# Attention and experts of a fused kernel: other homes for the state product, the fills, the splits and the router's numbers; conversion in half pieces, second half by row blocks

## The chip, the cores and the metric

The kernel runs on one core of one Trainium2 chip. The time is the device time of one execution in microseconds (us); a kernel is measured as the median of several runs. The core's engines are TensorE (PE in the profile, its weight loads PEld), VectorE (DVE), ScalarE (ACT), GpSimd (POOL) and SyncE (SP), which starts most DMAs. Products go from TensorE to the banks of PSUM; everything else lies in SBUF.

## The reference

Three layers stand one behind the other. The first is a gated linear recurrence over 768 steps for 2 x 8 heads of 40 numbers, the second a router with two of eight experts for 1,536 tokens of 320 numbers, the third a dense block with a SoLU, a norm and two more products.

```python
for t in range(S):                                  # attention, per batch and head
    m_new = max(f_gate + m, i_gate)
    f_stab, i_stab = exp(f_gate + m - m_new), exp(i_gate - m_new)
    C = f_stab * C + i_stab * outer(vt, kt); n = f_stab * n + i_stab * kt
    y[t] = sigmoid(o_gate) * (C @ qt) / max(abs(n @ qt), 1)
logits = x @ w_gate + log1p(exp(x @ w_noise)) * noise     # router, 8 experts
out[mask] += top2_w * (maximum(x[mask] @ w1[e], 0) @ w2[e])
h = x @ w_in; solu = h * softmax(h)                 # last block
return layer_norm(solu) * g_ln @ w_out
```

## The kernel before

**Attention** works in 12 tiles of 128 steps; tile i is of batch i % 2. Within a tile the recurrence is a masked product of scores, and the state `CC` carries what went before. One turn of the loop (line 684, i = 4 to 10) mixes work of several tiles: the router's ranks of tile i - 3, its numbers for tile i - 2, the rows of tile i - 1, the scores and keys of tile i + 1. `keys` gives GpSimd the product `qa` of the queries with the decay `A`, and VectorE the weighted keys `kw`. `update` multiplies keys and values to the bank `U`; `state` multiplies the old state by the decay of the tile's last step (line 388, on VectorE, `CC<-CC,A`) and adds the two halves of `U` (line 392). The next `update` may write the bank only behind those adds. `causal` masks a tile's `E` on GpSimd; `send` scatters a tile's rows to their experts by two indirect DMAs on GpSimd's queue.

**Fills** are matmuls on constant data, whose result nobody reads; in the prologue (up to 48.5 us: tiles 0 to 3, written out by hand in lines 531 to 682) they stand between the steps on TensorE. They write the columns 328 to 511 of the bank that `U` has at that moment.

**The router.** `trans` turns the rows into the bank pT (one buffer), `logits` writes 16 columns of it, `route_act` copies them to `lg` and takes a log of the noise half, `route` works on 8 numbers a token on VectorE, `slot` finds the place of the row. `weave` takes one step of each of several such chains in turn.

**Weights** come as f32 and are split into a high and a low part (`split_hi` on ScalarE, `split_lo`, line 121, on VectorE or GpSimd); a layer is then three matmuls for one. A raw tile `r0` to `r6` (0 to 2 are w1 by 1,024 columns, 3 to 6 are w2 by 640) may be loaded for the next expert (`load_w`) once both parts are made. The splits of expert 0 stand in the loop. Behind the loop (to 137.5 us) come the last tile's rows and router, and layer 1 and two of eight slices of layer 2 of expert 0's first 192 rows (`early_mm`, `early_cut`, `early_out`), then a branch on a count (line 801).

**An expert** (137.5 to 350.5 us, eight of them) has a first half, eight slices f of layer 1, each cut to high and low by ScalarE and VectorE (`cut_h`, lines 139 to 142), and a second half, layer 2 (lines 149 to 154), which runs over the slices f and within each over the row blocks n of 128 rows. Behind it `put` takes each block from PSUM (line 164) and scatters it. The last block's weights are 64-bit floats; `convert` makes f32 of them on VectorE, six pieces of 1,024 columns (w_out first), one step a slice in the second halves of the experts 1 to 6, over one buffer each of the raw tile `R`, `u`, `sc` and `sq`; the result in `u` is stored to DRAM (line 948). In code order the engines' queues are fixed; nothing is scheduled anew.

Of the kernel before, what the change touches and what calls it, by code (L numbers as in the profile page):

```python
# [36 lines left out]
def fused_kernel(ctx: ExitStack, tc, qt, kt, kv, og, ig, fg, wgn, noise, w1, w2, win, wout, gln, cst, out):  # L37
# [154 lines left out]
    with ExitStack() as pa:  # L192
# [56 lines left out]
        held = dict(U=pw)  # L249
# [132 lines left out]
        def state(i):  # L382
# [3 lines left out]
            Co, Cn, U = CC[b][c % 2], CC[b][(c + 1) % 2], T[i]["U"]  # L386
            if c > 0:
                ve.tensor_mul(Cn, Co, T[i]["A"][:, :, P - 1 : P].to_broadcast([P, 4, 82]))
# [39 lines left out]
        def route_act(i):  # L428
            lg = T[i]["lg"] = a2.tile([P, 16], F32, tag="lg", name=f"lg{i}")
            act.activation(lg, T[i]["pT"][:, 3, 0:16], AF.Copy)  # L430
            z = T[i]["z"] = a2.tile([P, NE], F32, tag="z", name=f"z{i}")
            act.activation(z, lg[:, 8:16], AF.Exp)
            act.activation(z, z, AF.Ln, bias=1.0)

        def route(i):
# [5 lines left out]
            yield ve.tensor_mul(z, z, noise_s[:, i])  # L441
            yield ve.tensor_add(z, z, T[i]["lg"][:, 0:8])
# [93 lines left out]
        fill(6)  # L536
# [3 lines left out]
        fill(6)  # L540
        for j in range(2):
            decays(1, j)
        fill(6)
# [17 lines left out]
        fill(8)  # L561
# [27 lines left out]
        fill(6)  # L589
        attend(0)  # L590
        fill(4)
# [21 lines left out]
        fill(6)  # L613
        trans(0)
        fill(4)
# [25 lines left out]
        fill(6)  # L641
        attend(2, 4, 8)
        fill(6)
# [34 lines left out]
        fill(6)  # L678
# [5 lines left out]
        for i in range(4, NTILE - 1):  # L684
# [13 lines left out]
            for j in (i - 5,) if i in (5, 7, 9) else (6,) if i == 10 else ():  # L698
                split_lo(0, j, pool)
# [8 lines left out]
            for j in (i - 5,) if i in (6, 8) else (5,) if i == 9 else ():  # L708
                split_lo(0, j, ve)
# [14 lines left out]
            for j in ((0, 1), range(2, 7))[i - CUT - 1] if i > CUT else ():  # L724
                load_w(1, j)
        t = NTILE - 1
# [24 lines left out]
        weave(route(t - 1))  # L751
        early_mm(0)
# [4 lines left out]
        weave(slot(t - 1))  # L757
        send(t - 1)
# [543 lines left out]
```

## Time and profile before

| what | before |
|---|---|
| median of 3 runs | 458.82 us (456.35 to 461.11) |
| profiled execution | 459.58 us, of which the span is 457.5 |
| mean granted clock of TensorE | 0.948 |
| busy: PE, DVE, ACT, POOL | 433.5 (95%), 297.1 (65%), 238.9 (52%), 191.8 (42%) us |
| DMA | 71.73 MB, 157 GB/s over the span |
| stages, us from the start | prologue to 48.5, loop to 106.8, behind it to 137.5, experts to 350.5, last block to 457.5 |

The busy share says which engine has the most work over all stages, not which one is waited for. The granted clock is the share of TensorE's full clock that the chip allowed in a stretch: 1.00 is 2.4 GHz, 0.50 is 1.2 GHz. In a row of instructions, the bracket is the engine's idle time just before it and who ended that.

### The profile page before, as it was taken

Reading aid. Unit: us, or ns where it says so; the run is one execution under the profiler, and the core shown is the slowest. Engines: PE = TensorE matmul, PEld = TensorE weight load, DVE = VectorE, ACT = ScalarE, POOL = GpSimd, SP = SyncE. Lnnn points to the kernel's source line nnn. Section 1 sums busy time; section 2 is a strip of 40 time slices with the busy share of each in tenths; the row PEclk is TensorE's granted clock in tenths of the full one; section 3 lists DMA queues with packets and bytes.
Section 4 is the critical chain, followed back from the end, with each engine's and each line's share of the span. In section 5 each row is a group of like instructions: output and inputs, shape, how many; then the busy total and the mean of one; then the engine's idle time right before and its main releaser. Section 6 shows DMA issues by size and latency. Waiting matters only on the chain.

```text
span 457.5 us, 8125 instructions
## 1 busy us (share of the span) xinstructions
PE 433.5 (95%) x2777; PEld 407.1 (89%) x2777; DVE 297.1 (65%) x722; ACT 238.9 (52%) x517; POOL 191.8 (42%) x277
## 2 busy tenths in 40 slices
PE   7998979999989999999999969979999999999996
PEld 4887979998978989899999969969999789989996
DVE  8696698797446558575647665486355877556541
ACT  4687574661327362644626156236382776665542
POOL 8534666676317250541807218045203253342340
PEclk9999785896599999999999998989999999999999
DMA  6777894664424947375483834834602411120001
GB/s 187 245 225 219 295 273 133 229 239 148 179 85 143 323 135 271 125 239 181 129 302 91 319 113 137 295 101 127 211 1 102 147 45 43 45 85 16 29 16 43
DMA packets 36094, 71.73 MB, mean 157 GB/s; under 512 B 4225, under 2 KB 18981, under 8 KB 35408
## 3 DMA queue, kind: packets, MB, share of 16 engines
q1 hardware_dynamic: 32896, 62.06, 42.3%
q0 software_dynamic: 2912, 8.68, 5.2%
q8 instruction: 24, 0.39, 0.4%
q10 hardware_dynamic: 240, 0.41, 0.3%
q14 instruction: 22, 0.18, 0.1%
HBM read 55.50 MB, written 16.21 MB: 157 GB/s over the span
## 4 chain that ended last, share of the span: by engine, by line
PE 51%; DVE 9%; DMA 5%; issue 3%; ACT 1%; DVEq 0%; ACTq 0%
PE cpo L1173 3%; PE cpo L1175 3%; PE cpo L1174 3%; PE ph L127 3%; DMA wi<-cvu 3%; PE po L149 3%; PE po L150 3%; PE po L151 3%; PE pz L1165 2%; PE ph L128 2%; PE ph L133 2%; PE ph L130 2%; PE ph L132 2%; PE ph L129 2%; PE ph L131 2%
## 5 line engine op out<-in xcount | busy, mean ns | idle before, releaser
L166 POOL DMA_INDIRECT yt<-YS,ti x29 | 28.9, 995 | 126.4 <-DVE YS L164 119.8
L140 DVE SCALAR_TENSOR_TENSOR h<-ph,h 128x384 fp32r<-128x384 f32 (+1 forms) x64 | 34.3, 537 | 39.6 <-ACT h L139 39.5
L121 POOL TENSOR_TENSOR w0l<-r,w0h 128x1024 fp32r<-128x1024 f32 x23 | 54.7, 2408 | 9.8 <-ACT w0h L117 9.5
L139 ACT ACTIVATE h<-ph 128x448 fp32r<-128x448 f32 (+6 forms) x64 | 32.0, 503 | 48.1 <-PE ph L134 47.5
L149 PE MATMUL po<-w1h,h 128*128 128x320 f32 x184 | 56.8, 308 | 0.0
L151 PE MATMUL po<-w1h,h 128*128 128x320 f32 x184 | 56.7, 308 | 0.0
L150 PE MATMUL po<-w1l,h 128*128 128x320 f32 x184 | 56.7, 308 | 0.0
L476 POOL DMA_INDIRECT xg<-x,slots x24 | 25.8, 1075 | 27.6 <-DVE ix L444 12.5
L149 PEld LDWEIGHTS po<-w1h,h 128*128 128x128 f32 x184 | 34.6, 188 | 0.0
L150 PEld LDWEIGHTS po<-w1l,h 128*128 128x128 f32 x184 | 34.6, 188 | 0.0
L151 PEld LDWEIGHTS po<-w1h,h 128*128 128x128 f32 x184 | 34.6, 188 | 0.0
L340 PE MATMUL S<-Qb,Kb 128*128 128x128 f32 x192 | 32.9, 310 | 0.0
L127 PE MATMUL ph<-XH,w0h 128*128 128x448 f32 (+6 forms) x64 | 24.5, 383 | 7.9 <-DVE h L142 4.8
L121 DVE TENSOR_TENSOR w1l<-r,w1h 128x640 fp32r<-128x640 f32 x34 | 31.3, 934 | 0.4 <-ACT w1h L117 0.4
L937 ACT ACTIVATE cvq<-cvR 128x1024 f32<-128x1024 f32 (+1 forms) x6 | 6.3, 1052 | 46.0 <-DMA cvR<-in_win_dram 27.2
L1167 DVE TENSOR_TENSOR ZL<-pz,ZH 128x512 fp32r<-128x512 f32 x24 | 15.4, 685 | 22.6 <-ACT ZH L1166 22.6
L1173 PE MATMUL cpo<-w1h,ZH 128*128 128x320 f32 x96 | 30.0, 312 | 0.0
L1175 PE MATMUL cpo<-w1h,ZL 128*128 128x320 f32 x96 | 29.7, 309 | 0.0
L1174 PE MATMUL cpo<-w1l,ZH 128*128 128x320 f32 x96 | 29.7, 309 | 0.0
L117 ACT ACTIVATE w0h<-r 128x1024 fp32r<-128x1024 f32 x27 | 28.2, 1051 | 0.0
L340 PEld LDWEIGHTS S<-Qb,Kb 128*128 128x128 f32 x192 | 27.6, 214 | 0.1
L380 PE MATMUL Y<-KV,E 128*128 128x41 f32 x192 | 27.0, 296 | 0.0
(266 smaller groups left out, 1262.2 us busy)
## 6 DMA issues: line engine op xcount, KB each, us to landing
r<-in_w_dram SPq DMA_DIRECT2D x24, 512.0 KB
r<-in_w_dram SPq DMA_DIRECT2D x32, 320.0 KB
E<-gd SPq DMA_DIRECT2D x8, 512.0 KB
X<-xg SPq DMA_DIRECT2D x7, 579.0 KB
KV<-in_kv_dram SPq DMA_DIRECT2D x12, 324.0 KB
cY<-yt SPq DMA_DIRECT2D x12, 320.0 KB
cvR<-in_win_dram SPq DMA_DIRECT2D x3, 1024.0 KB
cvR<-in_wout_dram SPq DMA_DIRECT2D x2, 1024.0 KB
```

The source lines that it names most:

```text
L121: eng.tensor_sub(splits[e][2 * m + 1][:, k : k + n], raws[e, j], splits[e][2 * m][:, k : k + n].bitcast(F32))
L127: pe.matmul(ph, W1H[:, 0, fs], XH[:, 0], start=True, stop=False)
L139: act.activation(h[:, 0:n], ph, AF.Relu)
L140: ve.scalar_tensor_tensor(h[:, n + r : n + r + w], ph[:, 0:w], 0.0, h[:, 0:w].bitcast(F32), op0=ALU.max, op1=ALU.subtract)
L149: pe.matmul(po, hh, W2H[:, f], start=a, stop=False)
L150: pe.matmul(po, hh, W2L[:, f], start=False, stop=False)
L151: pe.matmul(po, hl, W2H[:, f], start=False, stop=z)
L166: i = pool.indirect_dma_start(out=yt, out_offset=bass.IndirectOffsetOnAxis(ap=idx[0:w], axis=0), in_=YS[0:w], in_offset=None, bounds_check ...
L340: pe.matmul(S[:, a], Kb[i % 3][j][:, a], Qb[i % 3][:, a], start=True, stop=True)
L1173: pe.matmul(po, ZH[:, f], W2H[:, f], start=(f == 0), stop=False)
L1174: pe.matmul(po, ZH[:, f], W2L[:, f], start=False, stop=False)
L1175: pe.matmul(po, ZL[:, f], W2H[:, f], start=False, stop=(f == 7))
```

## The change

Attention: the state product goes from VectorE (in `state`) to GpSimd (in `keys`, a turn earlier). The 64 fills of 184 columns become 18 of 448: the first six in the warm-up's tile pw, the others in tiles of their own in the banks `pr` and `D`. `lg` is gone: `route_act` writes its logs to the bank pT, and `route` reads pT. Of the splits of expert 0, GpSimd makes the three of w1 in turns 5, 7 and 9, and VectorE the four of w2 behind the loop, each followed by the load of the next expert's piece (`split2`). Four slices of `early_out` go from behind the branch to ahead of it.

Experts: conversion in 11 pieces of 512 columns, `R`, `u` and `sq` with two buffers, pieces loaded two ahead; two pieces in each of the experts 1 to 6. The second half of the first seven experts runs over row blocks and within each over the slices; `put` follows each block, and ScalarE evicts the full ones. In code behind that, the last expert takes the names of the new buffers for its own tiles.

The fills:

```diff
-        held = dict(U=pw)
-        def fill(n):
+        def fill(n, tag="U"):
+            w = pw if tag == "U" else ps1.tile([P, 512], F32, tag=tag, name="fill")
             for _ in range(n):
-                pe.matmul(held["U"][:, 328:512], warm[:, 0:P], warm[:, 0:184], start=True, stop=True)
+                pe.matmul(w[:, 0:448], warm[:, 0:P], warm, start=True, stop=True)
...
-        fill(6)
+        fill(2)
...
-        fill(6)
+        fill(2, "pr")
...
-        fill(6)
+        fill(2, "D")
```

Keys, update, state:

```diff
                 pool.tensor_mul(T[i]["qa"], Qb[i % 3], T[i]["A"])
+                if c < NC - 1:
+                    pool.tensor_mul(CC[b][(c + 1) % 2], CC[b][c % 2], T[i]["A"][:, :, P - 1 : P].to_broadcast([P, 4, 82]))
...
-                held["U"] = ps1.tile([P, 512], F32, tag="U", name=f"U{i}")
-                U = T[i]["U"] = held["U"][0:104, 0:328].rearrange("p (a d) -> p a d", d=82)
+                U = T[i]["U"] = ps1.tile([P, 4, 82], F32, tag="U", name=f"U{i}")[0:104]
...
-            if c > 0:
-                ve.tensor_mul(Cn, Co, T[i]["A"][:, :, P - 1 : P].to_broadcast([P, 4, 82]))
```

Router:

```diff
-            lg = T[i]["lg"] = a2.tile([P, 16], F32, tag="lg", name=f"lg{i}")
-            act.activation(lg, T[i]["pT"][:, 3, 0:16], AF.Copy)
-            act.activation(z, lg[:, 8:16], AF.Exp)
-            act.activation(z, z, AF.Ln, bias=1.0)
+            act.activation(z, T[i]["pT"][:, 3, 8:16], AF.Exp)
+            act.activation(T[i]["pT"][:, 3, 32:40], z, AF.Ln, bias=1.0)
...
-            yield ve.tensor_mul(z, z, noise_s[:, i])
-            yield ve.tensor_add(z, z, T[i]["lg"][:, 0:8])
+            yield ve.tensor_mul(z, T[i]["pT"][:, 3, 32:40], noise_s[:, i])
+            yield ve.tensor_add(z, z, T[i]["pT"][:, 3, 0:8])
```

Splits of expert 0, in the loop and behind it:

```diff
-            for j in (i - 5,) if i in (5, 7, 9) else (6,) if i == 10 else ():
-                split_lo(0, j, pool)
+            if i in (5, 7, 9):
+                split_lo(0, i // 2 - 2, pool)
...
-            for j in (i - 5,) if i in (6, 8) else (5,) if i == 9 else ():
-                split_lo(0, j, ve)
...
+        def split2(j):
+            split_lo(0, j, ve)
+            load_w(1, j)
...
         weave(route(t - 1))
+        split2(3)
...
         weave(slot(t - 1))
+        split2(4)
...
         weave(rows2(t), route(t))
+        split2(5)
...
         weave(slot(t), totals())
+        split2(6)
...
+        for f in range(2, 6):
+            early_out(f)
```

Experts:

```diff
-        cvs = (3, 4, 5, 0, 1, 2)
+        CW = 512
+        cvs = [(wo32, wout, c) for c in range(0, 8 * DM, CW)] + [(wi32, win, c) for c in range(0, 3 * DFF, CW)]
...
+                R = raw[i] = b1.tile([P, CW, 2], I32, tag=f"R{i % 2}", name=f"cvR{i}")
...
-            u = b1.tile([P, DFF], I32, tag="u", name=f"cvu{i}")[:, :n]
+            u = b1.tile([P, CW], I32, tag=f"u{i % 2}", name=f"cvu{i}")
...
-            if i != cvs[-1]:
-                load_raw(cvs[cvs.index(i) + 1])
+            load_raw(i + 2)
...
-                put_y((e, n, 1), YS[n], pos[n], T3, X[e]["ti"][:, n : n + 1], ws[n] < P, act if n == 2 and e + 1 < NE else ve)
+                put_y((e, n, 1), YS[n], pos[n], T3, X[e]["ti"][:, n : n + 1], ws[n] < P, act if e + 1 < NE else ve)
...
-                for f in range(8):
-                    for n in range(len(ws)):
                         layer2(pos[n], splits[e], hs[f], f, n, n_e)
-                    if e > 0:
-                        next(cv, None)
-                    if f % 2 == 0:
-                        split(3 + f // 2)
-                for n in range(len(ws)):
+                cv = chain(*(convert(i) for i in range(2 * e - 2, min(2 * e, len(cvs))) if e > 0))
+                for n in range(len(ws)):
+                    for f in range(8):
                         layer2(pos[n], splits[e], hs[f], f, n, n_e)
+                        s = 8 * n + f
+                        if s % 3 < 2:
+                            next(cv, None)
+                        q = 6 if e > 0 else 3
+                        if s % q == 0 and s < 4 * q:
+                            split(3 + s // q)
                     put(n)
```

GpSimd in turn 7 of the loop, between its constant copy for one tile's rows and the mask. Before, with `qa` of tile 8, a split of expert 0 and the two scatters:

```order
L401 COPY x_1110<-consts 128x1
L350 TENSOR_TENSOR qa_1156<-Qb_149,A_1025 128x512
L121 TENSOR_TENSOR w0l_244<-r_2_873,w0h_243 128x1024
L475 MEMSET nop 1x1
L476 DMA xg<-x_892,slots 12288x386
L475 MEMSET nop 1x1
L476 DMA xg<-x_892,slots 12288x386
L333 AFFINE_SELECT E_976<-E_976 128x1024
```

And now:

```order
L400 COPY x_1058<-consts 128x1
L350 TENSOR_TENSOR qa_1104<-Qb_149,A_976 128x512
L352 TENSOR_TENSOR CC_160<-CC_159,A_976 128x328
L121 TENSOR_TENSOR w0l_244<-r_1_723,w0h_243 128x1024
L472 MEMSET nop 1x1
L473 DMA xg<-x_845,slots 12288x386
L472 MEMSET nop 1x1
L473 DMA xg<-x_845,slots 12288x386
L333 AFFINE_SELECT E_929<-E_929 128x1024
```

The state product stands between `qa` and the split (piece 1 of w1 where it was piece 2), with nothing between the three.

VectorE behind the loop, from the end of tile 10's `route` through its `slot` to tile 11's `route` (`sk`, `sf`, `slots`, then `z`). Before:

```order
L447 TENSOR_TENSOR mk_1625<-oh_1624 128x8
L448 TENSOR_TENSOR cum_93<-cum_92,mk_1625 128x8
L458 TENSOR_TENSOR sk_1663<-oh_1624,pr_1651 128x16
L459 TENSOR_REDUCE sf_1664<-sk_1663 128x2
L460 CAST slots<-sf_1664 128x2
L410 COPY x_1584<-x_1584 128x64
L441 TENSOR_TENSOR z_1648<-z_1648,noise_s 128x8
```

And now, where `r_3` and `r_4` are raw tiles of w2 of expert 0:

```order
L444 TENSOR_TENSOR mk_1551<-oh_1550 128x8
L445 TENSOR_TENSOR cum_93<-cum_92,mk_1551 128x8
L121 TENSOR_TENSOR w1l_246<-r_3_935,w1h_245 128x640
L455 TENSOR_TENSOR sk_1590<-oh_1550,pr_1578 128x16
L456 TENSOR_REDUCE sf_1591<-sk_1590 128x2
L457 CAST slots<-sf_1591 128x2
L121 TENSOR_TENSOR w1l_246<-r_4_1041,w1h_245 128x640
L409 COPY x_1510<-x_1510 128x64
L438 TENSOR_TENSOR z_1575<-pT_1542,noise_s 128x8
```

Two splits of 640 columns stand between these steps; the third stands behind tile 11's `route`, the fourth behind its `totals`. And `z` is read from pT.

VectorE at the end of one expert's second half and the start of the next (`h_0` and `h_1` are the first two cut slices). Before:

```order
L946 SCALAR_TENSOR_TENSOR cvu_3510<-cvs_3511,cvu_3510 128x1024
L947 SCALAR_TENSOR_TENSOR cvu_3510<-cvq_3512,cvu_3510 128x1024
L121 TENSOR_TENSOR w1l_3341<-r_6_3320,w1h_3340 128x640
L938 TENSOR_SCALAR cvu_3617<-cvR_3571 128x1024
L164 COPY YS_0_3494<-po_0_3490 128x320
L164 COPY YS_1_3495<-po_1_3491 128x320
L162 TENSOR_TENSOR YS_3_3497<-po_3_3493,T_3498 64x320
L140 SCALAR_TENSOR_TENSOR h_0_3656<-ph_0_3647,h_0_3656 128x384
L142 SCALAR_TENSOR_TENSOR h_0_3656<-ph_0_3647,h_0_3656 128x64
L140 SCALAR_TENSOR_TENSOR h_1_3669<-ph_1_3660,h_1_3669 128x384
```

And now:

```order
L943 SCALAR_TENSOR_TENSOR cvR_3847<-cvR_3847,cvs_4126 128x512
L944 TENSOR_TENSOR cvs_4126<-cvR_3847,cvs_4126 128x512
L947 SCALAR_TENSOR_TENSOR cvu_4125<-cvs_4126,cvu_4125 128x512
L121 TENSOR_TENSOR w1l_3907<-r_6_3858,w1h_3906 128x640
L948 SCALAR_TENSOR_TENSOR cvu_4125<-cvq_4127,cvu_4125 128x512
L162 TENSOR_TENSOR YS_3_4063<-po_3_4059,T_4064 64x320
L140 SCALAR_TENSOR_TENSOR h_0_4231<-ph_0_4222,h_0_4231 128x384
L142 SCALAR_TENSOR_TENSOR h_0_4231<-ph_0_4222,h_0_4231 128x64
L140 SCALAR_TENSOR_TENSOR h_1_4244<-ph_1_4235,h_1_4244 128x384
```

The two evictions of `po` are gone from VectorE's order, and so is the first operation of the next piece, which stood between the split and the evictions; the last operations of a half piece (512 columns) stand in its place.

## Rows read from the trace of the kernel before

**Rows 1.** Windows: us; busy us (count) of PE, PEld, DVE, ACT, POOL; PEclk, DMA share, GB/s

```profile
13.00:45.60 32.60, 29.00 (x271) 28.04 (x270) 24.78 (x71) 23.49 (x64) 13.88 (x21) 1.00 0.78 234
48.47:106.81 58.34, 55.11 (x409) 54.11 (x408) 50.25 (x172) 34.88 (x102) 37.81 (x48) 0.82 0.67 218
106.81:137.46 30.65, 28.55 (x170) 26.87 (x169) 15.46 (x91) 8.21 (x30) 10.77 (x21) 0.72 0.45 149
137.46:350.45 212.99, 204.97 (x1239) 196.09 (x1238) 131.83 (x256) 103.47 (x176) 81.26 (x80) 0.98 0.54 177
86.00:93.00 7.00, 7.00 (x65) 6.92 (x64) 5.44 (x26) 5.90 (x18) 3.89 (x6) 1.00 0.77 255
```

**Rows 2.** Windows, the stretches at half clock, columns as before

```profile
45.70:52.50 6.80, 6.30 (x34) 6.20 (x34) 3.85 (x22) 3.85 (x14) 4.37 (x8) 0.50 1.07 336
66.20:83.20 17.00, 16.68 (x81) 16.57 (x82) 14.40 (x50) 9.04 (x26) 10.11 (x12) 0.50 0.60 183
107.20:124.20 17.00, 17.00 (x80) 15.75 (x79) 9.34 (x49) 4.82 (x19) 8.32 (x16) 0.50 0.59 208
274.40:277.80 3.40, 3.40 (x12) 3.38 (x11) 1.71 (x6) 0.94 (x2) 2.93 (x6) 0.50 0.38 136
305.10:308.40 3.30, 3.30 (x12) 3.30 (x11) 1.52 (x3) 1.44 (x2) 2.84 (x6) 0.50 0.37 127
```

**Rows 3.** Waits of TensorE: engine, line, waited for, us in total, times, longest

```profile
PE ph L127 <- DVE h L142: 4.8, 3, 3.9
...
PE epo L149 <- PEq L801: 2.0, 1, 2.0
...
PE U L256 <- DVE CC L394: 1.5, 2, 1.0
```

**Rows 4.** Timeline: start, us, engine, line, operation, out<-in, shapes, count [idle before, ended by]

```profile
46.20 1.08 PE L256 MATMUL U<-warm 128*128 128x184 bf16 x6 [2.68 <-DVE CC L392]
...
62.50 3.27 DVE L388 TENSOR_TENSOR CC<-CC,A 128x328 f32<-128x328 f32 x1
...
64.15 1.25 POOL L350 TENSOR_TENSOR qa<-Qb,A 128x512 f32<-128x512 f32 x1
...
66.52 1.68 PE L367 MATMUL U<-KV,kw 128*104 128x82 f32 x8 [2.48 <-DVE CC L392]
```

**Rows 5.** Timeline of the experts, VectorE and TensorE around two waits for h

```profile
266.97 0.69 DVE L938 TENSOR_SCALAR cvu<-cvR 128x1024 int32<-128x1024 int32 x1 [6.64 <-DMA wi<-cvu]
267.58 0.82 DVE L121 TENSOR_TENSOR w1l<-r,w1h 128x640 fp32r<-128x640 f32 x1
...
274.06 0.42 PE L127 MATMUL ph<-XH,w0h 128*128 128x396 f32 x1 [3.89 <-DVE h L142]
...
304.39 0.44 PE L127 MATMUL ph<-XH,w0h 128*128 128x384 f32 x1 [3.09 <-DVE h L140]
```

**Rows 6.** Line 388: engine op xcount: ns min/median/max, first and last start, forms

```profile
L388 DVE TENSOR_TENSOR CC<-CC,A x8: 488/944/3278, 32.6 to 98.9; 128x328 f32<-128x328 f32 x8
```

**Rows 7.** Timeline of the prologue, the transposes of tile 1 and the add of tile 0's route

```profile
36.60 0.49 PE L416 MATMUL pT<-consts,x 128*128 128x128 f32 x3
...
36.90 0.16 DVE L442 TENSOR_TENSOR z<-z,lg 128x8 f32<-128x8 f32 x1
```

**Rows 8.** Timeline of TensorE in the loop, the update of two turns

```profile
87.37 0.88 PE L367 MATMUL U<-KV,kw 128*104 128x82 f32 x8
...
93.83 0.88 PE L367 MATMUL U<-KV,kw 128*104 128x82 f32 x8
```

**Rows 9.** Groups by shape, GpSimd, 46 to 106 us: count | busy us, mean ns | idle before

```profile
L121 POOL TENSOR_TENSOR w0l<-r,w0h 128x1024 fp32r<-128x1024 f32 x2 | 4.7, 2352 | 4.1 <-ACT w0h L117 4.1
```

**Rows 10.** Timeline of expert 0: two matmuls of layer 2, and the last slice's cut

```profile
169.87 0.30 PE L149 MATMUL po<-w1h,h 128*128 128x320 f32 x1
...
170.31 0.31 PE L149 MATMUL po<-w1h,h 128*128 128x320 f32 x1
...
170.65 0.56 DVE L140 SCALAR_TENSOR_TENSOR h<-ph,h 128x384 fp32r<-128x384 f32 x1 [0.64 <-ACT h L139]
```

More of the change, by code (lines that the diff above doesn't have):

```diff
@@ L539, in fused_kernel @@
         gates2(0, 1)
-        fill(6)
+        fill(2)
         for j in range(2):
             decays(1, j)
-        fill(6)
+        fill(2)
         exps(0)
@@ L560, in fused_kernel @@
         update(0)
-        fill(8)
         scores(1, 0)
@@ L588, in fused_kernel @@
         probs(1, 1)
-        fill(6)
+        fill(2, "pr")
         attend(0)
-        fill(4)
+        fill(2, "pr")
         for j in range(2):
@@ L612, in fused_kernel @@
         attend(1, 4, 8)
-        fill(6)
+        fill(2, "pr")
         trans(0)
-        fill(4)
         transc(0)
@@ L640, in fused_kernel @@
         attend(2, 0, 4)
-        fill(6)
+        fill(2, "D")
         attend(2, 4, 8)
-        fill(6)
+        fill(2, "D")
         trans(1)
@@ L677, in fused_kernel @@
         attend(3, 4, 8)
-        fill(6)
+        fill(2, "D")
         load_d(7)
@@ L723, in fused_kernel @@
                 early_load()
-            for j in ((0, 1), range(2, 7))[i - CUT - 1] if i > CUT else ():
+            for j in ((0, 1), (2,))[i - CUT - 1] if i > CUT else ():
                 load_w(1, j)
+        def split2(j):
+            split_lo(0, j, ve)
+            load_w(1, j)
         t = NTILE - 1
@@ L995, in prep_x @@
                 ve.tensor_sub(v["H"][64:128, d, 0:r], pt[64:128, 0:r], v["T"][64:128, 0:r].bitcast(F32))
-        def conversions():
-            for i in cvs:
-                yield from convert(i)
         X[0] = dict(x=rest, n=CAP - EARLY, w=[P] * ((CAP - EARLY) // P))
@@ L1008, in fused_kernel @@
         T3 = b1.tile([P, DM], F32, tag="T3", name="eT3")
-        for f in range(2, 8):
+        alloc_x(0)
+        for d in range(3):
+            prep_x(0, d)
+        for f in range(6, 8):
             early_out(f)
-            if f == 2:
-                alloc_x(0)
-            if f == 5:
-                for d in range(3):
-                    prep_x(0, d)
         for n in range(2):
             put_y((0, n), YS[n], early["po"][n], T3, eti[:, n : n + 1], n == 1, ve)
-        cv = conversions()
         for e in range(NE):
@@ L1041, in fused_kernel @@
                 if e == 0 and f == 7:
-                    load_raw(cvs[0])
+                    load_raw(0)
+                    load_raw(1)
                 if e + 1 < NE:
@@ L1070, in fused_kernel @@
             else:
-                tags = dict(Y="R", x2="u", XH="sc", XL="sq", T="T", pt="pt")
-                held = {}
+                tags = dict(Y=("R0", "R1", "Y2"), x2=("u0", "u1"), XH=("sq0",), XL=("sq1",), T=("T",), pt=("pt", "pt"))
                 def newb(t):
-                    def new(k, shape, dt):
-                        if k not in ("Y", "x2"):
-                            return (pst if k == "pt" else b1).tile(shape, dt, tag=tags[k], name=f"c{k}{t}")
-                        if k not in held:
-                            held[k] = b1.tile([P, 3 if k == "Y" else 2] + shape[1:], dt, tag=tags[k], name=f"c{k}")
-                        return held[k][:, t]
-                    return new
+                    return lambda k, shape, dt: (pst if k == "pt" else b1).tile(shape, dt, tag=tags[k][t], name=f"c{k}{t}")
                 for n in range(4):
```

19 lines of the change are left out of this document (8 added, 11 removed).

## The prediction, made before the change was run

> **What bounds the kernel now.** I read four views in this order. First, the busy time and granted clock by stage: in the experts (137.5 to 350.5 us) the profile has TensorE busy for 205.0 of 213.0 us at a mean clock of 0.98, while in the attention loop (48.5 to 106.8) the clock is 0.82 and in the stretch behind it (to 137.5) 0.72 [rows 1]. So TensorE sets the pace everywhere, but in attention it does so at half clock for much of the time: three stretches of 6.8, 17.0 and 17.0 us lie at 0.50, which is the 1.2 GHz level, and two of about 3.4 us lie in the experts, at 274.4 and at 305.1 [rows 2]. A half-clock stretch that TensorE fills costs half its length.
>
> Second, what TensorE waited for: nearly only VectorE. In the experts it waited for the cut of a hidden slice (`h`): 4.8 us in three waits [rows 3] and 3.09 in one that ended at 304.39 [rows 5]. In attention it waited for the state's add `CC`: 1.5 us in two waits ahead of the loop [rows 3], 2.68 us before 46.20 and 2.48 before 66.52 [rows 4]. So four of the five half-clock stretches begin at a long wait or within a microsecond of its end: 46.20, 66.52, 304.39, and 3.89 us before 274.06 [rows 5]; the third does not.
>
> Third, why VectorE was late. In attention it was the product `CC<-CC,A`, line 388, both of whose inputs lie in SBUF: 0.49 us at the least and 3.28 at the most [rows 6]. The one at 62.50 took 3.27 us; it ended 0.37 us after GpSimd's product `qa`, which had begun 1.65 us later [rows 4]. In the experts it was the conversion: at 266.97 VectorE had stood for 6.64 us because the next piece writes the one buffer `u` whose store to DRAM was still under way. Behind it in VectorE's order stood splits, two evictions of `po` and then the cut of `h`, so TensorE's layer 1 went on only at 274.06 [rows 5].
>
> **The change, part by part.**
>
> *Ahead of the loop.* Fills now write other banks (`pr`, `D`) than the U bank that the state add reads, so the waits of 1.5 us (two) and 2.7 us in front of fills go [rows 3, 4]. What comes next there is data that is ready: E of tile 0, x, logits. One new wait comes: `route` now reads its numbers from the one-buffer bank pT, so the transposes of tile 1 must wait for the add in `route(0)`, which ended at 36.90 + 0.16 = 37.06, where they began at 36.60 [rows 7]: 0.5 us, with scores of tile 4 queued behind. Fills come to 18 x 448 = 8,064 columns for 64 x 184 = 11,776; the 3,712 that go are 1.5 us at 2.4 GHz, a gain only where TensorE sets the pace, and VectorE is busy for 24.8 of 32.6 us beside it [rows 1], so I count them at nothing. Term: -4.2 + 0.5 = **-3.7**; bounds -5.2 (with the columns) and 0 (the other chains of the prologue take it all).
>
> *The loop, seven turns, 58.3 us.* At full clock a turn takes 93.83 - 87.37 = 6.46 us [rows 8], so seven take 45.2, the floor. The state product leaves VectorE (eight, 0.49 to 3.28 us) for GpSimd. GpSimd's price is bounded by its product over 512 columns (1.25 us, [rows 4]) and by nothing; in proportion 328 columns are 0.8 us, and I take 0.85, nearer to that row. GpSimd is busy 37.8 us in the loop [rows 1]; it gains five products (4.3) and a split of 1024 columns (2.35, [rows 9]), and loses one of 640 (in proportion about 1.5): 42.9, or 6.1 a turn, under 6.46 as a mean. In the turns 5, 7 and 9, which have a split, it has about 1.3 us more than a turn; causal masks are made a turn ahead, which covers one such turn but not three in full. So I take 48 us for the loop: the floor of 45.2 and 0.9 for each of those three. The wait of 2.5 us for the U bank goes with the long product, since the adds that free the bank (line 392) read PSUM and one SBUF tile. Term: 58.3 - 48 = **-10.3**; bounds -13.1 (floor) and -2 (one 17 us stretch at half clock again, 8.5).
>
> *Behind the loop, 30.7 us.* Four splits of 640 columns now stand in VectorE's order between route, slot and totals; undisturbed one takes 0.82 us [rows 5], together 3.3. VectorE is busy there for 15.5 of 30.7 us [rows 1], so they fit, yet they lie on the chain to the cuts that TensorE's `early_mm(6)` waits for. At half clock TensorE is the slower and they cost nothing; at full clock TensorE would be 8.5 us earlier, less some 2.5 of those splits, which gives -6. The stretch at half clock began here with no long wait ahead of it, only with small matmuls, and those stay; but VectorE comes in without the two delayed splits in turns 8 and 9. Between -6 and 0 I take **-2**, nearer to the row as it stands. The weight loads of expert 1 for layer 2 move behind these splits on SP's queue; they are wanted only in expert 0's second layer, over 10 us later. Four of the six early slices of layer 2 (20 matmuls, 2.9 us) move ahead of the branch; TensorE stands at it for 2.0 us [rows 3] wherever it comes, so this is a swap: 0. If the branch could hide behind them, -2.
>
> *Experts.* `u`, `sq` and the raw tile get two buffers, and raw pieces are loaded two ahead, so the wait for the store and the wait for the load go. Two half pieces are the work of one whole one plus seven more starts, on an engine that is busy 131.8 of 213.0 us there [rows 1]. Evictions of `po` go to ScalarE, one after each row block, so they no longer stand between VectorE and the next `h`. What is late next? A second half is 88 matmuls of 0.147 us = 12.9 us [rows 10]. Two half pieces are seven operations on 1024 columns in sum, between 0.69 us (the first of them) and twice that each: 5 to 10 us, and four splits 3.3 [rows 5]. At the upper bound VectorE ends some 0.4 us late, and the next `h` is wanted only three slices into the next layer 1: it fits. The row-block order asks for the last slice after 21 matmuls, 3.1 us; VectorE finished it at 171.2 with 169.87 as the start [rows 10], 1.3 us in. So all four waits go: 4.8 + 3.1 = 7.9, and with them the two half-clock stretches, half of 6.8 = 3.4. Term **-11.3**; bounds -11.3 and -4 (each second half waits one us for its last slice).
>
> *The two-input price.* The row of 3.27 us says: a VectorE operation with two SBUF inputs waits while GpSimd works back to back [rows 4]. Two such stay in each turn (`kw`, and x from nm and den). I add **+1.5** for them (bounds 0 and 8.4, below).
>
> *Sum.* -3.7 - 10.3 - 2 - 11.3 + 1.5 = -25.8 on the profiled execution's 459.58: 433.8. The runs' median, 458.82, lies 0.8 below it: **433**.
>
> The Trainium skill, "SBUF — State Buffer", section "Who interferes with whom", has a rule that speaks against this change: a VectorE instruction with two SBUF inputs contends with a GpSimd instruction that reads SBUF, and the later one is blocked in full. The rows of line 388 agree with it. By that rule the product on GpSimd does not end the contention but hands it to the next two-input operation, which would bring the sum to the time of rival 1 instead of 433.
>
> **Rivals.**
>
> 1. *GpSimd's longer run blocks VectorE again.* In turns 5, 7 and 9 GpSimd does `qa`, the new product and a split end to end: 1.25 + 0.85 + 2.35 = 4.4 us. A `kw` or an x that arrives at its start waits that long; VectorE's own work in a turn without such a wait is 5.4 us less the product's 0.5 [rows 1, 6], so some 1.6 us of a turn is slack. Three times (4.4 - 1.6) is 8.4 us: 433 + 8 - 1.5 = about 440; with one 17 us stretch at half clock after it, 449. For: line 388 shows the wait. Against: the product that waited stood in VectorE's order right before GpSimd's run of mask and `qa`, while `kw` and x stand earlier in a turn.
>
> 2. *All at full clock behind the loop too*: tail -6 and loop at its floor: 433 - 4 - 3 = 426; with the branch hidden, 424.
>
> 3. *Thin fills, slower.* Now the clock is full ahead of 45.6 us [rows 1]. If the thinner fills let it fall behind the third group of them, at 13 us, the 29.0 us of TensorE work from there to 45.6 [rows 1] would take twice as long: +29, less 2 us that TensorE waits anyway, so with the prologue's gain gone 433 + 4 + 27 = about 464, slower than before. It decides once more than 26 us of work runs at half clock. Against: the waits beside the fills go, so the stretch is fuller than before though its fills are fewer.
>
> 4. *Row blocks stall every second half; no change.* In the old order the last slice is wanted only in the last eighth of a second half, in the new one after 3.1 us of it. If VectorE brought it 3.6 us later than in the row at 170.65, TensorE would wait 1.8 us in each of seven second halves (12.6), and if each wait were followed by a half-clock stretch like that at 274.4 (half of 3.4 us, times seven, 11.9), the sum is 433 + 24.5 = about 457. For: a longer wait stood ahead of such a stretch at 274. Against: VectorE's order ahead of that cut holds no conversion.
>
> **How the numbers follow.** Forecast (427 to 440) 0.54; rival 1 (440 to 449) 0.20; rival 2 (418 to 427) 0.10; rival 4 (no change) 0.09; rival 3 (slower) 0.07. The range 422 to 449 holds the forecast, rival 1 and half of rival 2, 0.79. A measurement of this kernel can tell about 1% from no change: faster is forecast and rivals 1 and 2, 0.84, within it 0.09, slower 0.07.
>
> **What would show it.** Right: the experts' stage at 201 to 203 us with no wait of `ph` for `h` over 1 us, and no VectorE wait for the `cvu` store; `U` matmuls 6.5 to 7 us apart through the loop at a clock of 1.00; no fill waiting for `CC`; GpSimd over 85% busy in the loop. Wrong: `kw` or x rows of 2 us or more; a half-clock stretch ahead of 45 us or in the loop; GpSimd rows of the state product far over 0.85; TensorE waiting for `h` 3 us into a second half.

## The result and the profile after

The changed kernel takes 438.74 us (median of 4 runs, 438.07 to 441.10); the kernel before, run beside it, 459.13. The ratio is 0.957, its interval 0.951 to 0.963. Ratios that come with an interval (95%) leave out single runs that lie over 1.5% above the fastest run of their kernel. Forecast were 433 us and a range of 422 to 449. The profiled execution took 438.42 us, 436.6 of it span, with a mean granted clock of 0.963.

The stages below begin and end at the same instructions as those of [rows 1]: the first ranks matmul of the loop, that behind it, the first layer-1 matmul of expert 0, the end of the experts.

| stage | before, us | after, us | difference | term of the sum |
|---|---|---|---|---|
| ahead of the loop | 48.47 | 42.74 | -5.73 | -3.7 |
| loop | 58.34 | 55.83 | -2.51 | -10.3 + 1.5 |
| behind the loop | 30.65 | 28.91 | -1.74 | -2 |
| experts | 212.99 | 201.54 | -11.45 | -11.3 |
| last block | 107.05 | 107.58 | +0.53 | 0 |
| sum | 457.5 | 436.6 | -20.9 | -25.8 |

So the experts and the part behind the loop came to the size that was worked out, the prologue fell by more, and the loop kept 6.3 us that were to go. The windows of the changed kernel ("after" in what follows): three of the stages, then its two long stretches at half clock. Columns as in [rows 1].

```profile
42.74:98.57 55.83, 53.60 (x408) 52.39 (x407) 43.28 (x171) 34.48 (x100) 46.60 (x62) 0.85 0.76 247
98.57:127.48 28.91, 27.03 (x169) 25.98 (x169) 17.15 (x93) 7.53 (x27) 9.12 (x17) 0.76 0.52 152
127.48:329.02 201.54, 201.48 (x1239) 192.99 (x1238) 133.04 (x277) 110.11 (x195) 85.03 (x80) 1.00 0.58 187
52.60:69.70 17.10, 17.00 (x82) 16.72 (x83) 14.88 (x47) 6.91 (x20) 15.95 (x22) 0.50 0.70 237
103.80:117.40 13.60, 13.60 (x68) 13.33 (x68) 9.83 (x49) 3.59 (x13) 6.07 (x11) 0.50 0.66 206
```

In the experts TensorE is now busy for 201.48 of 201.54 us at full clock: no wait is left there to take away. Of the five half-clock stretches of [rows 2] two long ones remain, in the loop and behind it. What TensorE waited for in the whole of after, the longest sums:

```profile
PE pt L989 <- DVEq L804: 1.9, 1, 1.9
PE pw L250 <- DVE warm L232: 1.8, 1, 1.8
PE U L368 <- DVE CC L391: 1.8, 2, 1.5
PE pT L415 <- DVE den L403: 0.8, 1, 0.8
PE S L340 <- DVE E L344: 0.6, 2, 0.4
```

No wait for `h` is left, and no fill waits for `CC`; the branch (line 804) costs 1.9 us where it was 2.0 [rows 3]. One wait of 1.50 us for the U bank stands in the loop, right ahead of its half clock. The timeline of after shows where it came from, first GpSimd, then VectorE, then TensorE:

```profile
41.54 0.12 POOL L472 MEMSET nop<- 1x1 f32 x1
45.91 1.41 POOL L473 DMA_INDIRECT xg<-x,slots  x1 [4.25 <-DVE ix L441]
47.32 0.09 POOL L472 MEMSET nop<- 1x1 f32 x1
47.62 0.96 POOL L473 DMA_INDIRECT xg<-x,slots  x1 [0.21 <-issue]
48.59 1.11 POOL L333 TENSOR_SCALAR_AFFINE_SELECT E<-E 128x1024 f32<-128x1024 f32 x1
```

```profile
49.74 0.69 DVE L344 TENSOR_TENSOR E<-E,S 128x512 f32<-128x512 f32 x1 [2.82 <-POOL E L333]
50.34 1.72 DVE L357 TENSOR_TENSOR kw<-KV,wS 128x160 f32<-128x160 f32 x2
51.99 0.65 DVE L391 TENSOR_TENSOR CC<-CC,U 40x164 f32<-40x164 f32 x2
```

```profile
50.48 0.71 PE L340 MATMUL S<-Qb,Kb 128*128 128x128 f32 x4 [0.39 <-DVE E L344]
52.70 1.68 PE L368 MATMUL U<-KV,kw 128*104 128x82 f32 x8 [1.50 <-DVE CC L391]
```

GpSimd's first `send` (tile 0) stood for 4.25 us, though its slots were written at 40.94. The mask of tile 5 is queued behind it, so VectorE had nothing for 2.82 us; then the two `kw`, otherwise 0.31 us each, took 1.72 beside GpSimd's `qa` and state product; the add that frees the U bank came late, and from 52.64 the clock was at half for 17.1 us, which TensorE filled: 8.5 us. Later turns ran at or near their floor: the updates at 73.77, 80.23 and 86.69 us stand 6.46 apart, as in [rows 8]. The turns 7 and 9, in which GpSimd has a split, took 6.46 and 6.76 us from ranks to ranks.

### The profile page after: what moved, and what is told of

Same layout as the page of the kernel before. It is cut to its first block, busy times and chain, and to the rows that moved or that the text cites. A ratio compares the mean times of both kernels' runs of the same rounds, so it can differ in the third digit from the quotient of the medians.

```text
span 436.6 us, 8125 instructions
## 1 busy us (share of the span) xinstructions
PE 424.3 (97%) x2731; PEld 397.1 (91%) x2731; DVE 291.8 (67%) x736; ACT 242.9 (56%) x524; POOL 203.0 (46%) x284
## 4 chain that ended last, share of the span: by engine, by line
PE 70%; DVE 0%; ACT 0%; issue 0%; DVEq 0%; ACTq 0%
PE po L149 6%; PE po L151 6%; PE po L150 6%; PE ph L127 3%; PE cpo L1162 3%; PE cpo L1164 3%; PE cpo L1163 3%; PE ph L128 3%; PE ph L133 3%; PE ph L132 3%; PE ph L134 3%; PE ph L129 3%; PE ph L130 3%; PE ph L131 3%; PE pt L989 2%; PE pz L1154 2%
## 5 line engine op out<-in xcount | busy, mean ns | idle before, releaser
L121 POOL TENSOR_TENSOR w0l<-r,w0h 128x1024 fp32r<-128x1024 f32 x24 | 57.5, 2394 | 30.7 <-ACT w0h L117 27.5
L166 POOL DMA_INDIRECT yt<-YS,ti x29 | 31.2, 1075 | 86.1 <-ACT YS L164 55.7
L473 POOL DMA_INDIRECT xg<-x,slots x24 | 25.8, 1076 | 18.2 <-DVE ix L441 6.2
L121 DVE TENSOR_TENSOR w1l<-r,w1h 128x640 fp32r<-128x640 f32 x36 | 29.4, 821 | 2.6 <-ACT w1h L117 2.6
L164 ACT ACTIVATE YS<-po 128x320 f32<-128x320 f32 x20 | 8.8, 439 | 37.2 <-issue 31.1
L117 ACT ACTIVATE w1h<-r 128x640 fp32r<-128x640 f32 x36 | 25.5, 731 | 0.5 <-DMA r<-in_w_dram 0.5
L381 PEld LDWEIGHTS Y<-KV,E 128*128 128x128 f32 x192 | 25.1, 204 | 0.2
```

Of the source, the lines that this page charges most:

```text
L117: act.activation(splits[e][2 * m][:, k : k + n], raws[e, j], AF.Copy)
L121: eng.tensor_sub(splits[e][2 * m + 1][:, k : k + n], raws[e, j], splits[e][2 * m][:, k : k + n].bitcast(F32))
L166: i = pool.indirect_dma_start(out=yt, out_offset=bass.IndirectOffsetOnAxis(ap=idx[0:w], axis=0), in_=YS[0:w], in_offset=None, bounds_check ...
```

## The experiments

Medians are of 4 runs if nothing else is said. The kernel before took 460.63 us beside the first four experiments, 459.45 beside the next four and 462.22 beside the last three, so small differences go by the ratio to it; that of the changed kernel is 0.957.

**What held the first send.** First the order on GpSimd:

```diff
         keys(4)
-        send(0)
         state(3)
...
         causal(5)
+        send(0)
         logits(2)
```

> The changed kernel with one step moved on GpSimd: the first scatter of rows (send of tile 0) stands behind the mask of tile 5 and not ahead of it. Theory A (the send is in the way): in the changed kernel GpSimd stood until 45.91 us at that send, the mask and with it VectorE's product with the scores came 2.82 us late, TensorE waited 0.39 and 1.50 us, and the clock was at half for 17.1 us behind that, which is worth 8.5 us. Then the mask's wait on VectorE falls under 1 us, the stretch at half clock ahead of 70 us goes, the loop takes 45 to 48 us instead of 55.8, and the time is 428 to 431. Theory B (two SBUF inputs): the wait came because the two kw operations at 50.34 took 1.72 us beside GpSimd's qa and state product, whose place does not change; then the wait for the U bank and the half clock stay, 436 to 440. Theory C (the clock falls near 52 us whatever is waited for): the waits go, the half clock stays, 436 to 438.

438.89 us (434.13 to 440.81), ratio 0.958 [0.950, 0.965]. In its profile, which is the fastest of its runs (434.13), the loop takes 52.35 us; the waits of theory A are gone, and the 17 us stretch with them. The runs scatter, though, and the median didn't move. Another wait had come in the profile, at the first split:

```profile
57.45 2.33 POOL L121 TENSOR_TENSOR w0l<-r,w0h 128x1024 fp32r<-128x1024 f32 x1
...
57.55 2.26 DVE L444 TENSOR_TENSOR mk<-oh 128x8 bf16<-128x8 f32 x1
...
59.87 0.19 PE L449 MATMUL pr<-mk,ltri 128*128 128x8 bf16 x1 [2.12 <-DVE mk L444]
```

An add over 8 columns, 0.17 us in after, lasted until GpSimd's split was over ("held" in what follows): rival 1 as it was put, with `mk` in the place of `kw`, and half clock for 6.8 us from 58.72. So A holds for the first wait, and B is real, one turn later.

Why the send stood is told apart by a kernel that moves no work:

```diff
         keys(3)
+        for _ in range(8):
+            pool.memset(nop, 0.0)
```

> The changed kernel with eight one-element memsets added to GpSimd's order at a place where it is idle (behind keys of tile 3, 8 x 0.09 us): no work is moved, only the count of instructions ahead of the first send grows. The first send of the changed kernel started at 45.91 us, 4.25 us behind the instruction before it, with its inputs ready at 40.94 and 2.2 us behind the start of an 8 KB load of instructions at 43.67. Theory A1 (GpSimd waited for that load): the load falls into the idle time, the first send starts within 1 us of its predecessor, the mask of tile 5 comes in time, 428 to 433. Theory A2 (the send itself is late, for a DMA or another cause that has nothing to do with the count): the wait of over 4 us stays and so does 438 to 440.

433.84 us (433.30 to 437.03), ratio 0.949 [0.943, 0.956]: 0.8% below the changed kernel, for eight instructions more. The two intervals overlap, but each of the four runs is faster than each of the changed kernel's four. The send starts 0.16 us behind its predecessor:

```profile
42.13 0.12 POOL L472 MEMSET nop<- 1x1 f32 x1
42.41 1.23 POOL L473 DMA_INDIRECT xg<-x,slots  x1 [0.16 <-DVE x L442]
43.65 0.09 POOL L472 MEMSET nop<- 1x1 f32 x1
43.95 0.96 POOL L473 DMA_INDIRECT xg<-x,slots  x1 [0.21 <-issue]
45.30 1.09 POOL L333 TENSOR_SCALAR_AFFINE_SELECT E<-E 128x1024 f32<-128x1024 f32 x1 [0.39 <-ACT z L429]
```

An 8 KB packet of the instruction queue, which starts at 43.67 us in the changed kernel, starts at 33.98 in this one. The row of the view of DMA queues (packets, MB, share) in either window, 43.6 to 43.8 of after first, then 33.9 to 34.1 of the kernel with the memsets:

```profile
q14 instruction: 1, 0.01, 9.7%
```

```profile
q14 instruction: 1, 0.01, 13.5%
```

That a few instructions more on GpSimd move this packet by 9.7 us, into a time when GpSimd waits anyway, and take the stall away, is A1. In the changed kernel and in the ones with the old fills and with the send moved, the first send began 2.2 to 2.3 us behind the start of that packet (43.67 and 45.91; 47.19 and 49.38; 44.41 and 46.70); in the five other kernels below whose send stood for 4.4 to 5.5 us it began 2.2 to 2.4 us behind it. The loop is 49.15 us here, 6.7 less than in after; the prologue is 1.2 longer, with the clock at half for 3.4 us from 33.75.

```profile
43.98:93.13 49.15, 48.10 (x408) 47.33 (x408) 43.48 (x168) 34.25 (x100) 45.27 (x60) 0.93 0.83 273
```

How the stall becomes lost time differs from one execution to the next. The kernel with the order of slices undone (below) has the same attention code. In its profile the send stood for 4.39 us and TensorE waited 1.50 for the U bank, but the clock stayed full behind that. It fell at 61.9, for 6.8 us, where TensorE had waited 3.51 us more behind rows that were held beside GpSimd's product and split:

```profile
57.68 3.13 DVE L405 TENSOR_TENSOR x<-nm,den 128x320 f32<-128x320 f32 x1
...
58.13 2.33 POOL L121 TENSOR_TENSOR w0l<-r,w0h 128x1024 fp32r<-128x1024 f32 x1
...
60.96 0.52 PE L415 MATMUL pT<-consts,x 128*128 128x128 f32 x3 [3.51 <-DVE x L442]
```

The loop is 54.59 us there. So in these three profiles the loop takes 54.6 to 55.8 us with the stall and 49.15 without it: the stall costs 5 to 7 us, but that this must go by the half clock is not shown.

**The product.**

```diff
-                if c < NC - 1:
-                    pool.tensor_mul(CC[b][(c + 1) % 2], CC[b][c % 2], T[i]["A"][:, :, P - 1 : P].to_broadcast([P, 4, 82]))
...
+            if c > 0:
+                ve.tensor_mul(Cn, Co, T[i]["A"][:, :, P - 1 : P].to_broadcast([P, 4, 82]))
```

> The changed kernel with one part undone: the state product is on VectorE again, in state, as before the change; fills, router, splits and experts stay as changed. If the product's move carries most of the loop's term of the prediction (10.3 us forecast, 2.5 us seen), the time is 441 or more. Theory A (the send ahead of the mask sets the loop's stretch at half clock): the send stays where it is, so that stretch stays and the time is 438 to 442, the product's own durations being in VectorE's slack. Theory B (kw blocked by GpSimd's longer run is the cause): without the product GpSimd's run ends 0.9 us earlier, kw is shorter, the half clock goes, 430 to 433.

445.56 us (438.62 to 461.48), too scattered for an interval; by medians 0.967 of before. Two of the four runs, 447.36 and 461.48, make most of that; the mean of the other two, 441.2, is 0.961 of the mean of before without its two longest runs, some 2 us more than after. In the profile (443.76) the loop is 61.25 us, with VectorE busy for 54.43 of it (43.28 in after), since the product is held again, for up to 5.6 us, and TensorE waits 6.2 us in all for the U bank:

```profile
49.05 5.57 DVE L387 TENSOR_TENSOR CC<-CC,A 128x328 f32<-128x328 f32 x1
...
51.91 2.34 POOL L121 TENSOR_TENSOR w0l<-r,w0h 128x1024 fp32r<-128x1024 f32 x1
...
55.36 0.99 PE L366 MATMUL U<-KV,kw 128*104 128x82 f32 x4 [4.38 <-DVE CC L391]
```

The send did not stand here (0.28 us), so neither A nor B as written: three fewer instructions stand ahead of it, and the instruction packet came at 44.78 us, behind both first scatters. So the product's move does what it was made for, but it also shifted the packet into the way of the send; what it is worth in sum, 2 to 5 us, these runs don't settle. It is less than it was to carry.

**The long splits.**

```diff
-            if i in (5, 7, 9):
-                split_lo(0, i // 2 - 2, pool)
+            if i > 4:
+                j, o = (i - 5) // 2, (i - 5) % 2 * 512
+                pool.tensor_sub(splits[0][1][:, j, o : o + 512], raws[0, j][:, 0, o : o + 512], splits[0][0][:, j, o : o + 512].bitcast(F32))
```

> The changed kernel with one part altered: the three splits of 1,024 columns on GpSimd in turns 5, 7 and 9 are done as six of 512 columns in turns 5 to 10. Theory B (rival 1: an operation of VectorE with two SBUF inputs stands while GpSimd works on): no such operation can be held for longer than about qa, product and half a split; in the run with the send behind the mask one of them (mk, two inputs of 8 and 16 columns) took 2.26 us beside a split of 2.33. Then holds of over 2 us on VectorE's two-input rows disappear and the time is 430 to 437, as far as a held operation set TensorE's wait in the changed kernel. Theory A: the wait of turn 4 stands ahead of the first split, so the half clock from 52.6 us stays: 437 to 440.

439.22 us (438.12 to 442.11), ratio 0.958 [0.952, 0.964]: nothing gained, as theory A has it; the send still stood for 4.40 us. Nor did the holds of over 2 us go, as theory B had it: the cast of the slots took 2.66 to 2.74 us three times. With both edits:

> The changed kernel with both edits: the eight small memsets on GpSimd, and its splits in six halves of 512 columns over the turns 5 to 10. With the memsets alone the kernel took 433.84 us; its loop was 49.2 us, and beside the first split of 1,024 columns (54.41 to 57.02) an index cast of VectorE stood for 2.32 us. Theory B (what is left of the loop is VectorE held by the long splits): holds fall to 1.3 us or less in turn 5, the loop comes to 46 or 47 us, 430 to 432. Rival: GpSimd now has a piece in every turn, so some operation is held in each of six turns instead of three, and the loop stays at 49 or grows: 433 to 437.

432.27 us (430.71 to 436.61), ratio 0.941 [0.932, 0.951]: the lowest of all, below both kernels (with the changed one the intervals just touch); against the memsets alone the intervals overlap. In its profile the loop is 48.96 us and holds 3.4 us of half clock; the holds moved to the cast of the slots (median 1.56 us, at most 2.66, where it was 0.15 before the change). So theory B's loop of 46 to 47 didn't come.

**Fills.**

```diff
-            w = pw if tag == "U" else ps1.tile([P, 512], F32, tag=tag, name="fill")
-                pe.matmul(w[:, 0:448], warm[:, 0:P], warm, start=True, stop=True)
+                pe.matmul(held["U"][:, 328:512], warm[:, 0:P], warm[:, 0:184], start=True, stop=True)
```

> The changed kernel with one part undone: the 64 fills of 184 columns in the U bank are back. The prediction's term says that the waits in front of fills return: 4.2 us, so 443. By the columns alone 1.5 us: 440. If the other chains of the prologue set its length: 438.7 as now. The prologue (to the first ranks matmul of the loop) took 48.5 us before and 42.7 after; which of the three it is, shows in that mark, since a later start also changes how long the first send makes the mask wait.

444.03 us (442.94 to 446.10), ratio 0.967 [0.961, 0.972]: 4.4 us by the ratio. The prologue is 48.48 us again, as before: the fills carry its whole 5.7 us. (In this profile the loop is 2.8 us shorter than in after and the part behind it 4.2 longer, so the total is not the prologue's alone.) The prologue's waits for the state's adds are back,

```profile
PE U L257 <- DVE CC L393: 2.2, 1, 2.2
...
PE U L257 <- DVE CC L395: 1.7, 2, 1.1
```

3.9 us, and TensorE is busy for 42.40 us of the prologue where it is 39.30 in after:

```profile
0.00:48.48 48.48, 42.40 (x349) 36.86 (x349) 36.35 (x95) 29.59 (x76) 25.97 (x52) 1.00 0.73 219
```

```profile
0.00:42.74 42.74, 39.30 (x303) 33.12 (x304) 35.55 (x89) 28.38 (x73) 27.23 (x52) 1.00 0.78 233
```

The bank of the fills and their number were not undone apart; these rows alone tell the two shares.

**The experts.** Their part alone on the kernel before (the diff is that of the section on the change):

> The kernel before with the experts' part of the change alone: half pieces with two buffers, row blocks, evictions on ScalarE; attention as before. The stages of the changed kernel give 11.45 us for this part (213.0 to 201.5), so the time is 459.1 - 11.4 = 447 to 449, with no wait of TensorE for h over 1 us and a granted clock of 1.00 in the experts. Rival: part of the gain hung on attention's end (weights and rows that come earlier), then the experts keep a wait or a stretch at half clock and the time is 451 or more.

449.80 us (449.65 to 452.59), ratio 0.982 [0.975, 0.989], just above the 447 to 449 expected. The stage takes 201.67 us with TensorE busy for 201.55 at full clock, as in after: the part does not hang on attention. The median is 10.8 below that of before; the interval holds 11.4. Then each half undone in the changed kernel:

```diff
-                for n in range(len(ws)):
-                    for f in range(8):
+                for f in range(8):
+                    for n in range(len(ws)):
...
+                for n in range(len(ws)):
                     put(n)
```

> The changed kernel with one part of the experts undone: the second half of the first seven experts runs over the slices and within each over the row blocks again, the four evictions (on ScalarE) stand behind it; half pieces with two buffers stay. If the buffers carry the experts' 11.4 us, nothing returns: 438 to 440, and TensorE's stage of the experts stays at 201.5 us. If the order carries it (the evictions in one block at the end stand ahead of the next slices' cuts), each of seven second halves loses up to the four evictions, 4 x 0.44 us: 442 to 450.

438.24 us (438.17 to 446.09), ratio 0.957 [0.950, 0.963]; the stage 201.62 us. The order of rows and slices carries nothing.

```diff
-            u = b1.tile([P, CW], I32, tag=f"u{i % 2}", name=f"cvu{i}")
+            u = b1.tile([P, DFF], I32, tag="u", name=f"cvu{i}")[:, :n]
```

(and so for `R` and `sq`, one buffer each; pieces of 1,024 columns, loaded one ahead)

> The changed kernel with the other part of the experts undone: six whole pieces of 1,024 columns with one buffer each of R, u and sq, loaded one ahead; the row blocks and the evictions on ScalarE stay. If the buffers carry the gain, the waits for h return (4.8 and 3.1 us, and half of two stretches of 3.4): 447 to 450. If it was the evictions on VectorE that stood between the late conversion and the next cut, little returns: 439 to 442.

454.50 us (10 runs, 451.59 to 458.28), ratio 0.991 [0.987, 0.995]: more than all of it returns. The stage is 217.2 us, 4 us more than before the change, so with whole pieces and one buffer the new order, with its evictions on ScalarE, is worse than the old one. The wait of [rows 5] is back with its releaser, and so are TensorE's:

```profile
262.50 0.70 DVE L941 TENSOR_SCALAR cvu<-cvR 128x1024 int32<-128x1024 int32 x1 [6.08 <-DMA wi<-cvu]
```

```profile
PE ph L127 <- DVE h L140: 4.1, 1, 4.1
PE ph L127 <- DVE h L142: 3.8, 4, 2.6
PE ph L127 <- ACT w0h L117: 2.4, 1, 2.4
```

The buffers, with the smaller pieces and the earlier loads, carry the experts' gain; these three were undone together, not one by one.

**Splits and router.** The splits back in the loop (`split2` gone, VectorE's three at the end of turns 6, 8 and 9):

> The changed kernel with one part undone: the splits of expert 0 are as before, three of w1 and w2 on VectorE in turns 6, 8 and 9, four on GpSimd in turns 5, 7, 9 and 10, none behind the loop, and the loads of the next expert's w2 back at the end of turn 10. The prediction held the loop's gain to come from the product with the splits moved, and counted the four splits behind the loop at nothing. If so, the part behind the loop is as long as now (28.9 us, or 1 us less), the loop is longer by the three holds beside GpSimd (one took 3.29 us before the change): 440 to 447. If the splits don't matter in either place: 437 to 440.

442.07 us (441.15 to 443.16), ratio 0.960 [0.953, 0.967], which can't be told from 0.957. Its profile has both sides: the loop 59.37 us (a `kw` of 3.29 among the holds), 3.5 more than in after; the part behind it 27.95, 1.0 less, with 6.8 us at half clock where after has 13.6.

```diff
+            lg = T[i]["lg"] = a2.tile([P, 16], F32, tag="lg", name=f"lg{i}")
+            act.activation(lg, T[i]["pT"][:, 3, 0:16], AF.Copy)
...
-            yield ve.tensor_mul(z, T[i]["pT"][:, 3, 32:40], noise_s[:, i])
+            yield ve.tensor_mul(z, z, noise_s[:, i])
```

> The changed kernel with one part undone: route_act copies the logits to lg again, and route reads lg and z from SBUF. The prediction gave this edit one cost (0.5 us, once, for the bank pT) and no gain of its own. By the holds seen in the changed kernel it has one: two more operations a tile with two SBUF inputs can be held by GpSimd, and a copy more stands on ScalarE. If that matters, 440 to 446; if not, 437 to 439.

447.97 us (442.21 to 452.52), by medians 0.969 of before. Two runs, 452.18 and 452.52, make that; the mean of the other two, 443.0, is 0.961 of the mean of before without its two longest runs, which can't be told from 0.957. So no gain of the router's edit is shown by the times. The profile (442.21) shows why it may have one: the two operations that read SBUF again are held (ns, min/median/max), while in after neither takes more than 0.17 us:

```profile
L441 DVE TENSOR_TENSOR z<-z,lg x12: 149/154/2997, 34.5 to 113.3; 128x8 f32<-128x8 f32 x12
L440 DVE TENSOR_TENSOR z<-z,noise_s x12: 155/383/2607, 34.0 to 113.1; 128x8 f32<-128x8 f32 x12
```

In its profile the prologue is 1.1 us shorter than in after (41.63), the loop 2.5 longer (58.37), the part behind it 2.3 longer (31.21); the first send, reached earlier, stood for 5.46 us.

## Why the prediction was right, and where it was not

- **Experts, -11.3: right in size and cause.** -11.45. The store's wait through one buffer made `h` late, and comes back with one buffer and whole pieces; half pieces in two buffers take it away without the row blocks, which I let carry part of it and which carry nothing. Rival 4 (row blocks stall) didn't occur: no wait for `h` stands in the list of after.
- **Prologue, -3.7: the mechanism right, the term too small.** The waits came back with the old fills (3.9 us, 4.2 forecast). I counted the fills that go at nothing because VectorE was busy beside them; they are 3.1 us of TensorE's time (42.40 less 39.30), twice the 1.5 that I had from their columns. The new wait for the bank pT costs 1.1 us by the profile of the router's experiment (41.63 against 42.74) where I had 0.5.
- **Loop, -10.3: the step that failed.** The floor of 6.46 us a turn held, and GpSimd's price held (0.74 us median and 1.05 at most; I took 0.85). What failed is the step from there to 48 us: that GpSimd would keep up, with 0.9 us for each of three turns, and that the wait for the U bank would go. The product made GpSimd's instruction stream such that a load of it fell on the first send, which no row of before showed. In the profile of after, 2.2 us of waits and 8.5 of half clock are the gap between 45.2 and 55.8. The stall is taken away by the memsets, and the loop is then 49.15. This was the bound "one 17 us stretch at half clock again", reached by a cause that I didn't name: that the range and the forecast's own band held is luck in this part, with the prologue's 2.0 us too many against the loop's miss. The 0.9 us for each turn with a split were 0 and 0.3 in the full-clock turns. GpSimd was busy for 46.6 us where the sum gives 42.9, since two more scatters and one more `qa` and mask fell into the loop.
- **The two-input price, +1.5, and rival 1.** The mechanism is there, and it moves rather than ends, as the rival says: `kw` up to 1.53 us, x up to 3.14 in after (a sign of being wrong by the prediction's own list), `mk` 2.26 with the send moved. It cost less than the rival's 8.4 in the profile of after, where the longest hold lay in the half-clock stretch and TensorE did not wait for it; with the same attention code at full clock it cost a wait of 3.51 us. I listed two operations a turn that can be held; there are more. The rival's price was also too high: the 5.4 us of VectorE's work are those of a window of 7.00 us, 5.0 in a turn of 6.46, which gives 7.2 for 8.4. And one detail of the rule that the prediction quotes does not fit the rows: it is not only the later of two that is blocked. The product at 49.05, back on VectorE in its experiment, had begun before GpSimd's mask (49.51), `qa` (50.69) and split (51.91), and ended 0.37 us behind the last of them; so did the row of 62.50 [rows 4]. In these rows a held operation waits for the end of GpSimd's unbroken run.
- **The router, given no gain.** With both numbers in PSUM, two operations a tile were not held in after (0.17 us at most), which were held for up to 3.0 us with the numbers in SBUF. The prediction left this out; a gain in time is not shown.
- **Behind the loop, -2.** -1.74, but not for the clock: with the send moved the stage ran at a mean clock of 0.94 and took 27.74 us, 1.2 less than in after, so rival 2's 6 us weren't there. TensorE stands at the branch for 1.9 us as it did, now with two slices behind it in place of six: the swap that was counted at 0. With the four splits back in the loop the part was 1.0 us shorter, but also at half clock for 6.8 us less, so what they cost here stays open.
- **Rival 3 (thin fills)** didn't occur: the clock is 1.00 up to 52.6 us in after, with 18 fills for 64. Two other profiles with these fills have 3.4 us at half clock in the prologue (with the memsets from 33.75, with whole pieces from 33.21); so has one with the old fills, twice (the experts' part alone, from 22.65 and 36.31), so these don't hang on the thinner fills alone.

What is left open: why the clock fell at 103.84 in after, where no wait over 1 us stands ahead (as at 107.13 before); why it fell behind the wait of 1.50 us in some profiles and not in others; and why single runs of one kernel differ by up to 5% (438.62 to 461.48) where holds on VectorE and GpSimd are many.

## What to carry to other kernels

Half pieces in two buffers, where one buffer waited for its store, gave what the waits in the trace said, and fewer fills, in banks that nobody else waits for, gave more than that. Moving an operation between two engines that hold each other up moves the hold with it: list every operation that can be held, down to casts of two columns. Small operands in PSUM were not held here; what that is worth in time was not shown. And a wait that no semaphore explains may be the instruction stream itself: a few instructions more, in an idle place, can show it.

## What the hardware showed that was not expected

- **An engine can stand for its instructions.** GpSimd idled 4.25 us with its inputs ready, until 2.2 us behind the start of an 8 KB instruction packet, at a time when the DMA engines were busy (share 1.07 between 40 and 46 us); eight extra instructions in an idle time moved the packet by 9.7 us, and the median was 4.9 us lower. The Trainium skill, "Runtime: NRT & Kernel Launch", section "Instruction fetch mechanics", says that the sequencer fetches the next block while it executes the current one and that this is mostly hidden; here one such load was not. That the busy DMA engines are the reason is not shown.
- **Casts are held too.** The cast of two columns `slots<-sf` took 0.15 us before at the median and 0.17 at most, and up to 2.72 in after, at 54.20, beside GpSimd's mask and `qa` (54.39 to 56.84); the index cast took 2.32 with the memsets, beside the split. The Trainium skill, "SBUF — State Buffer", section "Who interferes with whom", says of copies and casts, too, that they can contend with GpSimd; I had read it for two-input operations alone. These casts agree with it.

```profile
L460 DVE CAST slots<-sf x12: 143/148/169, 42.8 to 125.3; 128x2 int32<-128x2 f32 x12
```

```profile
L457 DVE CAST slots<-sf x12: 146/168/2716, 39.8 to 113.8; 128x2 int32<-128x2 f32 x12
```

The rows give the count, the shortest, median and longest duration in ns, and the first and last start, in the kernel before and in after.
